# Two-item gelu, third-level sums, early output products for the last tokens, and a re-tuned planner, in an attention kernel with an MLP beside it

## Chip, cores, metric

One core of one Trainium2 chip. The metric is device time in microseconds (us) of one execution. A kernel before and a kernel after are compared on the same chip, in alternation. The profiled span is 1.7 to 2.2 us shorter than the time measured for the same execution. Engines are called PE (matmul), PEld (its weight loads), ACT (ScalarE), DVE (VectorE), POOL (GpSimd) and SP (SyncE, which issues the transfers).

## The reference

```python
# x: (1, 2048, 1024) bf16, 32 heads of 32; w1: (1024, 3584), w2: (3584, 1024)
def reference(A_x, A_wqkv, A_wo, B_x, B_w1, B_b1, B_w2, B_b2):
    xn = _layernorm(A_x)
    s = attention(xn, A_wqkv) @ A_wo                 # softmax(q k / sqrt(32)) v, all 2048 x 2048 pairs
    y = _layernorm(xn)
    h = jax.nn.gelu(y @ B_w1 + B_b1, approximate=True)
    g = jax.nn.silu(h @ B_w2 + B_b2)
    return A_x + s * g
```

## The kernel before

The attention is cut into 512 units: 8 head groups of 4 heads, 8 query blocks of 256 tokens, 8 pairs of key blocks. A unit is 8 score matmuls on PE, two exps of 128x1024 on ACT, then products with V and with a block of ones (the row sums) on PE. DVE first adds the P tiles (the results of the exps) pairwise, so that fewer products with ones are needed. The MLP and the projections fill PE's time between scores, in chunks of one or a few matmuls. An instruction that takes a finished result out of PSUM is called an evacuation; the prologue is the normalisation of x and the first projections. A Python planner, which runs when the program is built, simulates the engines with a few constants and fixes the instruction order of each engine. On the chip every engine then takes its instructions in that order.

```python
# planner: how long a transfer takes (in ns), and what issuing one costs SP
state["bw"] = max(state["bw"], t) + o.nbytes / 210.0
o.fin = state["bw"] + 1900.0
...
def dma(sem, fn, nbytes, R, W, prio=3, extra=()):
    return add("SP", fn, 70, 0, R, W, prio, sem=sem, nbytes=nbytes, extra=extra)
...
# one w1 item: 16 matmuls in chunks of two, then gelu over its 512 columns
for k in range(8):
    ...
    chunk(it, fn, 2 * Q256, [("w1", gi), ("yT", k % 4)])
dve(... xb_t[i3] = bank + b1T ...)                      # out of PSUM
dve(... sq = xb * xb ...); dve(... ut = (sq + 1/GA) * xb ...)
act(lambda e: e.activation(ut_t[i3][:], ut_t[i3][:], ACT.Tanh, scale=GC * GA), c_act(512), ...)
dve(... hT = (ut + 1) * xb ...)
...
# row sums: two levels of adds for each pair of units; either is dropped if it would be late
pa = dve(... PA[u], PA[u+1] = P[:, :, 0] + P[:, :, 1] ...)   # 2048 columns
pb = dve(... PA[u] = PA[u] + PA[u+1] ...)                    # 1024 columns
...
# output of 128 tokens x 512 columns: eight products, one evacuation, one add, one store.
# For the last 256 tokens the eighth (head group 7) is kept apart and may start first in its bank.
for hc in range(HG):
    chunk(itb if hc == 7 else it, fn, Q512, ...)
```

The softmax here doesn't subtract the row's maximum and nothing guards it: scores larger than these inputs give would overflow.

## Time and profile before

| | kernel before |
|---|---|
| time, median of 3 runs | 1062.07 us (1061.9 to 1062.5) |
| span of the profiled execution | 1060.2 us |
| end of the last exp | 1046.1 us |
| tail: last exp to last PE / PE to the end | 10.7 + 3.4 us |
| full 512-wide matmuls after the last product with V, in PE's order | 43 |

The busy shares, the chain and the stretches are shown in the prediction. Two more views: first the waits of PE, with the columns total us, times, longest us (the nine that follow these are of 0.5 to 2.2 us each, for results of DVE, POOL and ACT).

```profile
PE ps L1058 <- ACT P L1067: 8.0, 18, 1.2
PE ps L668 <- issue: 3.5, 22, 0.2
```

Then the transfers of w1, by count, size and median us from issue to landing. The planner took 524288 / 210 + 1900 = 4397 ns for one with no other ahead of it, which is the measured median as the view rounds it.

```profile
w1r<-in_B_w_dram SPq DMA_DIRECT2D x112, 512.0 KB, 4.4
```

One measure is used throughout. ACT starts its next instruction 904 ns after an exp (a copy, at 920, is counted alike), 520 after a tanh of 512 columns, 946 after one of 1024; what a start comes later than that is its lateness. From 62 us on I call a start *long late* if it is over 0.18 us late, and *brief* is the sum of all the rest. Before, long late starts make 0.2 us and brief ones 10.6; up to 62 us ACT loses 17.9 (*opening*).

### The profile page before, as it was taken

Reading aid. Unit: us, or ns where it says so; the run is one execution under the profiler, and the core shown is the slowest. Engines: PE = TensorE matmul, PEld = TensorE weight load, DVE = VectorE, ACT = ScalarE, POOL = GpSimd, SP = SyncE. Lnnn points to the kernel's source line nnn. Section 1 sums busy time; section 2 is a strip of 40 time slices with the busy share of each in tenths; the row PEclk is TensorE's granted clock in tenths of the full one; section 3 lists DMA queues with packets and bytes.
Section 4 is the critical chain, followed back from the end, with each engine's and each line's share of the span. In section 5 each row is a group of like instructions: output and inputs, shape, how many; then the busy total and the mean of one; then the engine's idle time right before and its main releaser. Section 6 shows DMA issues by size and latency. Waiting matters only on the chain.

```text
span 1060.2 us, 32647 instructions
## 1 busy us (share of the span) xinstructions
PE 1026.5 (97%) x14502; PEld 643.7 (61%) x14562; DVE 946.9 (89%) x1585; ACT 1028.9 (97%) x1186; POOL 31.2 (3%) x42
## 2 busy tenths in 40 slices
PE   7999999999999999999999999999999999999998
PEld 5756466556665566566665566466665666665443
DVE  8479898999999998899989998999999998978996
ACT  4999999999999999999999999999999999999994
POOL 5500000000000000000000000000000000000000
PEclk9999999999999999999999999999999999999999
DMA  9335166522674466423763476224765776662442
GB/s 268 111 96 158 42 179 190 144 76 71 186 207 126 113 193 196 113 57 112 206 192 105 122 199 195 74 76 121 212 180 151 221 217 190 179 197 70 134 140 87
DMA packets 285798, 156.52 MB, mean 148 GB/s; under 512 B 23642, under 2 KB 276570, under 8 KB 285658
## 3 DMA queue, kind: packets, MB, share of 16 engines
q1 hardware_dynamic: 285658, 154.44, 51.0%
q8 instruction: 114, 1.87, 0.8%
q14 instruction: 26, 0.21, 0.1%
HBM read 142.35 MB, written 12.06 MB: 146 GB/s over the span
## 4 chain that ended last, share of the span: by engine, by line
ACT 93%; PE 4%; DVE 2%; DMA 1%; issue 0%; SPq 0%; POOL 0%; POOLq 0%
ACT P L1067 86%; ACT ut L939 5%; PE ps L668 3%; ACT gw L971 2%; DVE stats L823 1%; DMA hT<-in_A_x_dram 1%; PE ps L663 1%; ACT big L814 0%; PE ps L1058 0%; PE ps L803 0%; DVE yT L911 0%; POOL gw L847 0%; DVE V L740 0%; DVE mv L825 0%; SPq L693 0%
## 5 line engine op out<-in xcount | busy, mean ns | idle before, releaser
L1067 ACT ACTIVATE P<-ps 128x1024 bf16<-128x1024 f32 x1024 | 986.8, 1243 | 5.3 <-PE ps L1058 5.3
L1087 DVE TENSOR_TENSOR PA<-P 128x2048 bf16<-128x2048 bf16 x243 | 294.7, 1215 | 25.4 <-ACT P L1067 24.1
L668 PE MATMUL ps<-yT,w1r 128*128 128x256 bf16 x1792 | 234.9, 275 | 2.3 <-DVE xb L931 1.1
L668 PE MATMUL ps<-w2r,hT 128*128 128x256 bf16 x1792 | 226.9, 273 | 0.3 <-DVE nv L1121 0.2
L668 PEld LDWEIGHTS ps<-yT,w1r 128*128 128x128 bf16 x1792 | 162.1, 98 | 60.5 <-issue 28.6
L668 PEld LDWEIGHTS ps<-w2r,hT 128*128 128x128 bf16 x1792 | 162.2, 98 | 51.0 <-issue 30.5
L1091 DVE TENSOR_TENSOR PA<-PA 128x1024 bf16<-128x1024 bf16 x219 | 147.7, 684 | 1.4
L663 PE MATMUL ps<-P,V 128*32 128x256 bf16 x4096 | 142.8, 274 | 0.6 <-DVE xb L931 0.4
L668 PE MATMUL ps<-big,qk 128*128 128x512 bf16 (+2 forms) x522 | 120.9, 357 | 5.7 <-issue 2.1
L668 PE MATMUL ps<-qk,big 128*128 128x256 bf16 (+1 forms) x723 | 121.2, 305 | 2.5 <-issue 1.3
L663 PEld LDWEIGHTS ps<-P,V 128*32 128x32 bf16 x4096 | 97.7, 96 | 33.1 <-issue 19.6
L1058 PE MATMUL ps<-QKT 32*128 32x256 bf16 x2048 | 101.7, 273 | 7.4 <-ACT P L1067 5.9
L1058 PE MATMUL ps<-qk 32*128 32x256 bf16 x2048 | 101.9, 273 | 6.2 <-ACT P L1067 2.1
L939 ACT ACTIVATE ut<-ut 128x512 f32<-128x512 f32 x112 | 94.5, 855 | 0.0
L668 PEld LDWEIGHTS ps<-qk,big 128*128 128x128 bf16 x736 | 65.3, 98 | 41.5 <-issue 13.3
L931 DVE TENSOR_TENSOR xb<-ps,b1T 128x512 bf16<-128x512 f32 x112 | 76.6, 684 | 13.9 <-PE ps L668 12.6
L941 DVE SCALAR_TENSOR_TENSOR hT<-ut,xb 128x512 bf16<-128x512 f32 x112 | 76.4, 684 | 5.9 <-ACT ut L939 5.2
L668 PEld LDWEIGHTS ps<-big,qk 128*128 128x128 bf16 x568 | 47.7, 98 | 52.4 <-issue 15.6
L1058 PEld LDWEIGHTS ps<-QKT 32*128 32x128 bf16 x2048 | 30.3, 92 | 76.6 <-ACT P L1067 75.9
L937 DVE SCALAR_TENSOR_TENSOR ut<-sq,xb 128x512 f32<-128x512 bf16 x112 | 76.1, 682 | 0.3
L1058 PEld LDWEIGHTS ps<-qk 32*128 32x128 bf16 x2048 | 30.4, 92 | 71.6 <-ACT P L1067 67.4
L663 PE MATMUL ps<-PA,ones 128*32 128x256 bf16 x1068 | 56.0, 274 | 0.3 <-DVE PA L1091 0.3
(75 smaller groups left out, 532.2 us busy)
## 6 DMA issues: line engine op xcount, KB each, us to landing
w1r<-in_B_w_dram SPq DMA_DIRECT2D x112, 512.0 KB, 4.4
w2r<-in_B_w_dram SPq DMA_DIRECT2D x128, 448.0 KB, 4.4
qk<-in_A_wqkv_dram SPq DMA_DIRECT2D x16, 256.0 KB, 3.2
g_scratch<-gw SPq DMA_DIRECT2D x32, 128.0 KB, 3.0
o_scratch<-ot SPq DMA_DIRECT2D x56, 64.0 KB, 2.8
big<-o_scratch SPq DMA_DIRECT2D x28, 128.0 KB, 3.5
hT<-in_A_x_dram SPq DMA_DIRECT2D x10, 256.0 KB, 5.5
qk<-in_A_wqkv_dram SPq DMA_DIRECT2D x4, 512.0 KB, 4.4
```

Source lines behind the costliest of these rows:

```text
L663: ins = e.matmul(dst(j), lhsT=lhsT(j), rhs=rhs(j), start=start, stop=stop, tile_position=(0, 32 * j), skip_group_check=True)
L668: return e.matmul(dst, lhsT=lhsT, rhs=rhs, start=start, stop=stop, skip_group_check=True)
L823: dve(lambda e, t=t, c=c: e.bn_stats(stats[:, t, c, :], xst[t][:, c * 512:(c + 1) * 512]), 600, [XS(t)], [("st", t, c)], 1)
L931: dve(lambda e: e.tensor_tensor(xb_t[i3][:].rearrange("p (k t) -> p k t", k=2), bank(it.bank).rearrange("p (k t) -> p k t", k=2), b1T[:, 2 ...
L937: dve(lambda e: e.scalar_tensor_tensor(ut_t[i3][:], sq_t[p % 2][:], 1.0 / GA, xb_t[i3][:], op0=ALU.add, op1=ALU.mult), c_f32(512), [("sq", ...
L939: act(lambda e: e.activation(ut_t[i3][:], ut_t[i3][:], ACT.Tanh, scale=GC * GA), c_act(512), [("ut", i3)], [("ut", i3)], 1)
L941: dve(lambda e: e.scalar_tensor_tensor(hT[:, hs].rearrange("p k t -> p (k t)"), ut_t[i3][:], 1.0, xb_t[i3][:], op0=ALU.add, op1=ALU.mult), ...
L971: act(lambda e: e.activation(zh_t[zi], z_t[zi], ACT.Tanh, scale=0.5), c_act(512), [("z", zi)], [("zh", zi)], 1)
L1058: ins = e.matmul(bank(b0[j], kk * 256, (kk + 1) * 256), lhsT=QKT[sl][32 * j:32 * j + 32, 1, kb * 128:(kb + 1) * 128], rhs=QKT[sl][32 * j:3 ...
L1067: x = act(lambda e, h=h: e.activation(P[pi][:, 2 * h:2 * h + 2].rearrange("p j k q -> p (j k q)"), ps[:, pr[h] * 1024:(pr[h] + 1) * 1024], ...
L1087: pa = dve(lambda e: e.tensor_tensor(PA_all[:, a0:a0 + 2].rearrange("p u j q -> p (u j) q"), P_all[:, p0:p0 + 2, :, 0, :].rearrange("p u j ...
L1091: pb = dve(lambda e: e.tensor_tensor(PA[a0][:], PA[a0][:], PA[a1][:], op=ALU.add), c_b16(1024), [("PA", a1)], [("PA", a0)], PBPRIO)
```

## The change

Four things at once:
- **Gelu over two w1 items**: the squares, the cubic step and the tanh work on 1024 columns instead of twice 512; the gate (silu) likewise. ACT saves fixed costs.
- **A third level of sums**: four units share one product with ones where DVE is in time.
- **The last 256 tokens**: their products of head groups 0 to 6 are made earlier and kept in f32; only the eighth product stands at the end.
- **The planner**: new constants for transfers and latencies, chunks of one matmul, three x tiles ahead of the first weights, other patience and reserve values, and a rule ("suspension") by which one item of the prologue may go ahead of an opened one.

```diff
-GRACE2 = 600     -HARD = 45    -EARLY = 6    -RESERVE = 300    -GLAST = 11    -NOPA = 24
+GRACE2 = 1200    +HARD = 40    +EARLY = 3    +RESERVE = 800    +GLAST = 13    +NOPA = 0
+FINE = 1   +XF = 3   +ADJ = 300   +PART = 5   ...
-                state["bw"] = max(state["bw"], t) + o.nbytes / 210.0
+                state["bw"] = max(state["bw"], t) + o.nbytes / 280.0
...
-            return add("SP", fn, 70, 0, R, W, prio, ...)
+            return add("SP", fn, 430, 0, R, W, prio, ...)
...
-            for k in range(8):
-                f2, dcs = k // 4, (2 * (k % 4), 2 * (k % 4) + 1)
+            for k in range(16 // FINE):
+                f2, dcs = k // (8 // FINE), [FINE * (k % (8 // FINE)) + i for i in range(FINE)]
...
-            act(lambda e: e.activation(ut_t[i3][:], ut_t[i3][:], ACT.Tanh, scale=GC * GA), c_act(512),
+            if p % 2 == 0:
+                return it
...
+            act(lambda e: e.activation(ut_t[i2][:], ut_t[i2][:], ACT.Tanh, scale=GC * GA), c_acts(1024),
...
+            add8 = dve(lambda e: e.tensor_tensor(PA[a0], PA[a0], PA[a2], op=ALU.add), c_b16(1024),
+                       [("PA", a2)], [("PA", a0)], PCPRIO)
...
+                if qb == PART:
+                    for t2 in range(2):
+                        wo_load(NQB - 1, t2)
+                        for nh in range(2):
+                            wo_item(NQB - 1, t2, nh, 0, 7)     # products of head groups 0 to 6, kept in f32
```

(Constants set side by side and cuts marked with "...".)

## The prediction

> **What bounds the kernel now.** I read the busy shares first, then the chain that ended last, then ACT's starts, then the two ends of the run.
>
> ```profile
> PE 1026.5 (97%) x14502; PEld 643.7 (61%) x14562; DVE 946.9 (89%) x1585; ACT 1028.9 (97%) x1186; POOL 31.2 (3%) x42
> ...
> ACT 93%; PE 4%; DVE 2%; DMA 1%; issue 0%; SPq 0%; POOL 0%; POOLq 0%
> ```
>
> PE and ACT tie at 97%, so busy time does not decide between them. The chain does: 93% of the span is ACT, mostly the 1024 exps. The stretches say when:
>
> ```profile
> core 0: us, PE busy (x) PEld busy (x) DVE busy (x) ACT busy (x) POOL busy (x), PEclk, DMA share, GB/s
> 12.70:62.00 49.30, 44.82 (x584) 32.64 (x585) 32.35 (x83) 41.83 (x45) 26.49 (x32) 0.97 0.48 138
> ...
> 250.00:500.00 250.00, 246.56 (x3554) 159.26 (x3559) 230.95 (x381) 250.00 (x291) 0.00 (x0) 1.00 0.50 140
> ...
> 1046.00:1060.30 14.30, 10.66 (x80) 5.00 (x79) 7.49 (x15) 0.08 (x1) 2.31 (x2) 1.00 0.21 74
> ```
>
> In the middle ACT has no idle time at all (250.00 of 250). It loses time only before 62 us, and after 1046 us it has nothing left to do. So three things set the time: how early ACT becomes dense, how much ACT work there is, and the tail after the last exp.
>
> What one ACT instruction costs is the distance between starts, not its recorded length, because neighbours overlap:
>
> ```profile
> 400.48 0.87 ACT L939 ACTIVATE ut<-ut 128x512 f32<-128x512 f32 x1
> 401.01 4.01 ACT L1067 ACTIVATE P<-ps 128x1024 bf16<-128x1024 f32 x4
> 404.62 0.91 ACT L939 ACTIVATE ut<-ut 128x512 f32<-128x512 f32 x1
> 405.14 6.80 ACT L1067 ACTIVATE P<-ps 128x1024 bf16<-128x1024 f32 x7
> ```
>
> The 512-wide tanh is recorded with 0.87 us but holds ACT for 401.01 - 400.48 = 0.53; over all such pairs in the trace the median is 520 ns for the gelu tanh and for the gate's alike. Four exps fill 404.62 - 401.01 = 3.61, or 0.90 each (median 904 ns).
>
> I also took the excess of every exp start over 904 ns. From 62.5 us on, the first exps of a pair are late 131 times for 8.2 us in all, and each late one starts about 50 ns after the last matmul of its scores: ACT waits there for PE, too briefly to show as idle. The PE work just ahead of those scores is half the time (4.1 of 8.2 us) an MLP chunk of two 256-wide matmuls.
>
> **What the Trainium skill says.** "ScalarE: Activation LUTs", section "What ACT_TABLE_LOAD costs", gives 186 ns + 0.833 ns per column for an ACTIVATE with immediate scale and bias, with neighbours overlapping by about 93 ns. That leaves 93 + 0.833 x 512 = 520 ns per 512-wide tanh: the trace agrees to the nanosecond. For the exp from PSUM it would give 946 and the trace has 904, so I use the trace there. "VectorE: DVE Perf Modes", section "Side-by-side: where the cycles go for N=2048 bf16", puts a two-times-mode bf16 operation of 2048 columns at about 1224 ns; the trace has 1215 for the sums of that size, and 684 for 1024 columns. The fixed part of one DVE instruction is therefore worth saving, but only if DVE matters. "TensorE: Matmul & The Clock Gate", section "Back-to-back issue gap", has N/2.4 + 2.5 for warm isolated matmuls, 216 ns at N=512; in the tail the trace has 215 or 216 between every two of them (the same section's 131 ns for streams is not what this trace shows).
>
> **The change, part by part.** Counts are from the order in which the two built programs stand.
>
> ACT: 112 gelu tanhs of 512 become 56 of 1024, 32 gate tanhs become 16. The columns stay; 72 fixed parts of 93 ns go: 72 x (2 x 520 - 946) = 72 x 94 ns = 6.8 us. The 946 is an estimate from the skill's formula, which held at 512. ACT is the bound where this happens, so nearly all of it should come off the end: **-6.8 us**.
>
> DVE:
>
> ```profile
> L1087 DVE TENSOR_TENSOR PA<-P 128x2048 bf16<-128x2048 bf16 x243 | 294.7, 1215 | 25.4 <-ACT P L1067 24.1
> L1091 DVE TENSOR_TENSOR PA<-PA 128x1024 bf16<-128x1024 bf16 x219 | 147.7, 684 | 1.4
> L663 PE MATMUL ps<-PA,ones 128*32 128x256 bf16 x1068 | 56.0, 274 | 0.3 <-DVE PA L1091 0.3
> L663 PE MATMUL ps<-P,ones 128*32 128x256 bf16 x208 | 7.1, 273 | 0.0
> ```
>
> First-level sums go 243 to 251, second-level 219 to 202, and 57 third-level sums are new. In distances between starts (1135 ns for 2048 columns, 602 for 1024 bf16 or 512 at the single rate, 335 for 512 bf16): +8 x 1.135 - 17 x 0.602 + 57 x 0.602 = +33.2 us. The two-item gelu gives back 56 x (2 x 0.335 - 0.602) = 3.8 for the squares, 56 x (2 x 0.602 - 1.135) = 3.9 for the cubic step, and 16 x 0.07 = 1.1 for the gate; the last gelu step stays split. DVE thus gains about 24 us of work, from 89% to some 92% busy by the page's measure. It is beside ACT, so I count **0**, but it takes slack away.
>
> PE: matmuls against ones fall from 1276 to 1052, that is 224/4 = 56 groups of four at about 0.11 us (the tail has 28 of them in some 0.8 us): 6 us less. PE is not the bound, so **0** directly. Chunks of the MLP and of V become one 256-wide matmul (0.11 us) instead of two: a score matmul can be late by one such matmul less. If that and the corrected model of latencies halve the 4.1 us behind MLP chunks and take a little of the rest: **-2.5 us**, the softest term.
>
> Start: POOL normalises without a pause from 13 to 38 us in the kernel before, and the order of those instructions is the same after, so the end of the prologue does not move. What moves is how ACT fills it. Before, 10 exps stand ahead of its last copy out of PSUM, after it 12: one pair, 1.8 us, done in time that was idle. Before, one pair also waits 1.1 us at 61 us because 12 MLP matmuls stand ahead of its scores; that should be gone, but the new order can have such a place elsewhere. **-2.5 us**.
>
> Tail:
>
> ```profile
> 1046.34 1.10 PE ps L663 x36
> 1047.43 0.16 issue
> 1047.59 9.24 PE ps L668 x42
> 1056.83 0.03 issue
> 1056.86 0.70 DVE w1r L1221
> 1057.56 0.02 issue
> 1057.58 0.43 DVE w1r L1228
> ```
>
> Making the last tokens' seven products early sounds like taking 28 matmuls out of this stretch. The order says otherwise: after the last product with V there stand 43 full matmuls before and 45 after. The early products went in front, and the products of the 256 tokens ahead of them slid behind in their place. So PE needs 2 x 0.216 = 0.43 us more, and 20 fewer matmuls with V or ones (36 to 16) save about 0.6. But the end behaves worse. The last five matmuls now finish five different output tiles within 0.86 us. DVE takes five evacuations at 0.60 from 0.82 before the last matmul's end, then one bf16 add at 0.34 and two f32 adds, the last of 0.68: -0.82 + 5 x 0.60 + 0.34 + 0.60 + 0.68 = 3.8 us after the last matmul, where before it is 58.01 - 56.82 = 1.2. The store after it takes the same 2.2 us. Together 0.4 - 0.6 + 2.6: **+2.5 us** (rounded).
>
> Sum: -6.8 - 2.5 - 2.5 + 2.5 = -9.3 us on a span of 1060.2, or 1050.9; the measured time lies 1.9 above the span (1062.07 against 1060.2), so 1052.8, which I round to 1052.5.
>
> **Rivals.** (1) DVE or the deeper chain of sums becomes a wait. A third-level sum is ready only after three dependent DVE instructions, and PE takes its order as it stands: if a sum is late, PE stops with score matmuls behind it and ACT starves. For it: DVE at 92%, and PE already waits some 3 to 4 us in total for second-level sums. Against it: the program drops 70 of 127 possible third-level sums, as it does where they would be late, and the products they feed come after most of a later exp group. This would cost 5 to 10 us: 1057 to 1062. (2) PE takes over, so that a shorter ACT stream does nothing. For it: 97% busy. Against it: PE busy is lengths that overlap, and weight loads ahead of scores wait for exps 490 times (143 us in total), so PE has room. If it were so, only the 6 us of ones would count: about 1056. (3) Finer chunks remove all late scores and the prologue closes: another -5 and -3, about 1044. (4) The tail really shortens by the 28 matmuls, 6 us: it would need the other products done before the last exp; the order speaks against it. About 1046.
>
> **Range and chances.** ACT's terms are firm, the other three are each good to 2 or 3 us, and rivals 1 and 3 pull in opposite directions: 1045 to 1059.5. Faster by over 2% means under 1040.8. The ACT floor is 1024 x 0.904 + 72 x 0.946 + 16 copies at about 0.9 = 1008, plus 8.2 before the first copy, some 8 of gaps and a tail of 14: 1038 at best, so hardly. Slower by over 2% would take a large new wait.
>
> **What would show it.** Right: 56 and 16 tanhs with 946 ns to the next start; ACT without idle time between about 50 and 1037 us; DVE near 970 us busy; last exp near 1035 to 1038; a tail of 16 to 17 us with five evacuations in a row. Wrong: a merged tanh that holds ACT for 1040 ns; exps late by more than 8 us in all; PE waiting for third-level sums just ahead of scores; a tail under 13 us.

## The result, and the profile after

The kernel after takes 1066.96 us (median of 4 runs, 1065.52 to 1067.59), the kernel before 1062.28 (4 runs, 1061.9 to 1063.47). Ratios here are the mean time of one kernel's runs over that of the other's of the same rounds, so not quite the ratio of the medians that are quoted: 1.004, with a 95% interval of 1.0023 to 1.0058. By the 2% rule that is the same; but the change was predicted to save 9.6 us (1062.07 - 1052.5) and costs about 4. The result lies outside the predicted range.

The page of the kernel after, busy shares and the chain that ended last:

```profile
PE 1024.6 (96%) x14338; PEld 637.8 (60%) x14338; DVE 977.4 (92%) x1513; ACT 1024.3 (96%) x1114; POOL 34.0 (3%) x42
...
ACT 46%; PE 45%; DVE 4%; DMA 3%; POOL 1%; issue 0%; DVEq 0%; POOLq 0%
```

The chain was 93% ACT; now 45% of it runs over PE, and 3% over transfers. The stretches (length, then busy us of PE, PEld, DVE, ACT, POOL, then PE clock, DMA share, GB/s):

```profile
250.00:500.00 250.00, 245.92 (x3527) 156.77 (x3525) 228.26 (x341) 248.37 (x272) 0.00 (x0) 1.00 0.50 141
...
750.00:967.00 217.00, 211.90 (x3062) 140.70 (x3050) 198.49 (x295) 215.23 (x236) 0.00 (x0) 1.00 0.65 188
```

ACT had no idle time in these stretches before (250.00 and 217.00 busy). Now it stands idle 1.6 and 1.8 us, and 2.8 from 62 to 250 us. PE's waits say for what:

```profile
PE ps L1116 <- ACT P L1125: 11.3, 22, 2.4
PE ps L705 <- DMA w1r<-in_B_w_dram: 6.0, 6, 1.7
PE ps L705 <- DVE xb L976: 2.3, 5, 0.8
```

The middle line is new: six times PE stands before the first matmul of a w1 item until its weights have landed. One of them in the timeline (start, length, engine, line; in brackets the idle time before it and what ended it):

```profile
908.13 1.36 PE L705 MATMUL ps<-yT,w1r 128*128 128x256 bf16 x11 [1.68 <-DMA w1r<-in_B_w_dram]
...
909.42 0.40 PE L1116 MATMUL ps<-qk 32*128 32x256 bf16 x8
...
909.87 1.02 ACT L1125 ACTIVATE P<-ps 128x1024 bf16<-128x1024 f32 x1 [1.47 <-PE ps L1116]
```

PE waits 1.68 us, works off the 11 matmuls that stand before the next scores in its order, and ACT, which needs those scores, is idle 1.47 us. It is not the only one: after five of the six waits (5.4 us) a long late start follows within 2 us, and these five make 6.1 of the 9.8 us of long late starts in this execution. The transfers themselves have not slowed, since the median is 4.5 us against 4.4. What has changed is what the planner believes: 524288 / 280 + 1900 = 3772 ns. When a weight is needed as soon as it lands, it now places PE's first matmul 0.63 us before the median landing. Taken from the traces, the time from landing to first matmul of the 112 items was 17.4 us in the median before, and once as short as 0.14 us, which is what it is when PE stands waiting; after, the median is 11.5, and ten items are at 0.14.

The merged tanh, and the second-level and new third-level sums (busy us, mean ns):

```profile
L1151 DVE TENSOR_TENSOR PA<-PA 128x1024 bf16<-128x1024 bf16 x202 | 137.9, 689 | 1.7
...
L991 ACT ACTIVATE ut<-ut 128x1024 f32<-128x1024 f32 x56 | 67.6, 1212 | 0.0
...
L1154 DVE TENSOR_TENSOR PA<-PA 128x1024 bf16<-128x1024 bf16 x57 | 39.3, 689 | 1.3
```

By distance between starts a merged tanh holds ACT for 947 ns, so the predicted 946 holds. The end of the chain (start, us, what):

```profile
1048.33 8.97 PE ps L705 x41
...
1057.32 0.69 DVE V L1266
1058.02 2.39 DVE w1r L1266 x4
1060.41 0.84 DVE V L1269
1061.25 0.60 DVEq L1356
1061.85 0.60 DVE w1r L1271
```

Five evacuations in a row, then the adds, as predicted. The last matmul ends at 1058.15 us (a group of five that starts at 1056.91 and takes 1.24), the last DVE instruction at 1061.85 + 0.60 = 1062.45: 4.3 us, not 3.8. The tail comes to 17.3 us against 14.1. The timeline of the same place shows why the one bf16 add is long:

```profile
1058.69 2.27 POOL L1271 TENSOR_TENSOR w1r<-w1r,hT 128x512 bf16<-128x512 bf16 x2 [1013.92 <-DVE w1r L1266]
...
1060.32 0.93 DVE L1269 TENSOR_TENSOR V<-V 128x512 bf16<-128x512 bf16 x1
```

It takes 0.93 us, where the same instruction took 0.42 at 1056.32 us, alone. It ends 0.29 us after POOL's two adds do (1058.69 + 2.27 = 1060.96). The Trainium skill has such a case in "SBUF — State Buffer", section "Who interferes with whom": a DVE instruction with two SBUF inputs contends with a GpSimd instruction that reads SBUF. The trace agrees, with 0.5 us; the evacuations, which have one input in PSUM, ran on beside POOL at 0.60 us each. How long one engine holds the other up is not shown here, since spans on POOL are rough.

### The profile page after: what moved, and what is told of

It reads as the page before. It is cut to its first block, busy times and chain, and to the rows that moved or that the text cites. A ratio compares the mean times of both kernels' runs of the same rounds, so it can differ in the third digit from the quotient of the medians. Undisturbed runs are those within 1.5% of the kernel's fastest.

```text
span 1064.9 us, 32134 instructions
## 1 busy us (share of the span) xinstructions
PE 1024.6 (96%) x14338; PEld 637.8 (60%) x14338; DVE 977.4 (92%) x1513; ACT 1024.3 (96%) x1114; POOL 34.0 (3%) x42
## 4 chain that ended last, share of the span: by engine, by line
ACT 46%; PE 45%; DVE 4%; DMA 3%; POOL 1%; issue 0%; DVEq 0%; POOLq 0%
ACT P L1125 43%; PE ps L705 30%; PE ps L1116 8%; PE ps L700 7%; DMA w1r<-in_B_w_dram 3%; ACT ut L991 3%; DVE ut L860 1%; DVE PA L1146 0%; ACT gw L1027 0%; POOL gw L889 0%; POOL lnp L903 0%; DMA hT<-in_A_x_dram 0%; DVE xb L976 0%; DVE V L777 0%; DVE PA L1151 0%
## 5 line engine op out<-in xcount | busy, mean ns | idle before, releaser
L1125 ACT ACTIVATE P<-ps 128x1024 bf16<-128x1024 f32 x1024 | 960.9, 1198 | 10.8 <-PE ps L1116 10.5
L1146 DVE TENSOR_TENSOR PA<-P 128x2048 bf16<-128x2048 bf16 x251 | 303.9, 1212 | 17.1 <-ACT P L1125 15.9
L705 PE MATMUL ps<-yT,w1r 128*128 128x256 bf16 x1792 | 232.4, 273 | 8.7 <-DMA w1r<-in_B_w_dram 6.0
L700 PE MATMUL ps<-P,V 128*32 128x256 bf16 x4096 | 146.0, 275 | 0.9 <-DVE V L777 0.5
L1151 DVE TENSOR_TENSOR PA<-PA 128x1024 bf16<-128x1024 bf16 x202 | 137.9, 689 | 1.7
L705 PE MATMUL ps<-big,qk 128*128 128x512 bf16 (+2 forms) x568 | 131.2, 361 | 2.6 <-DVE V L777 0.8
L705 PE MATMUL ps<-qk,big 128*128 128x256 bf16 (+1 forms) x736 | 124.9, 306 | 0.2
L989 DVE SCALAR_TENSOR_TENSOR ut<-hT,xb 128x1024 f32<-128x1024 bf16 x56 | 68.2, 1220 | 0.1
L991 ACT ACTIVATE ut<-ut 128x1024 f32<-128x1024 f32 x56 | 67.6, 1212 | 0.0
L1200 DVE STREAM_TRANSPOSE nt<-ps 128x256 f32<-128x256 f32 x64 | 28.7, 448 | 28.2 <-PE ps L700 27.9
```

What stands on the lines that cost most here:

```text
L700: ins = e.matmul(dst(j), lhsT=lhsT(j), rhs=rhs(j), start=start, stop=stop, tile_position=(0, 32 * j), skip_group_check=True)
L705: return e.matmul(dst, lhsT=lhsT, rhs=rhs, start=start, stop=stop, skip_group_check=True)
L989: dve(lambda e, r=r: e.scalar_tensor_tensor(ut_t[i2][:, r], h[:, r], 1.0 / GA, xb[:, r], op0=ALU.add, op1=ALU.mult), c_f32(r.stop - r.star ...
L991: act(lambda e: e.activation(ut_t[i2][:], ut_t[i2][:], ACT.Tanh, scale=GC * GA), c_acts(1024), [("ut", i2, 0), ("ut", i2, 1)], [("ut", i2, ...
L1125: x = act(lambda e, h=h: e.activation(P[pi][:, 2 * h:2 * h + 2].rearrange("p j k q -> p (j k q)"), ps[:, pr[h] * 1024:(pr[h] + 1) * 1024], ...
L1146: add2.append(dve(lambda e, p0=p0, a0=a0: e.tensor_tensor(PA_all[:, a0:a0 + 2].rearrange("p u j q -> p (u j) q"), P_all[:, p0:p0 + 2, :, 0 ...
```

## The experiments

All sixteen runs were correct. Every call ran on one chip beside the kernel before (median 1060.84, 1060.79, 1060.72 and 1061.53 us, 7 to 9 runs each). The columns: span; end of the last exp; tail as PE + rest; lateness in the opening; long late starts from 62 to 110 us and after 110; PE's waits for w1; full matmuls after the last product with V; ratio to the kernel before with its interval. "-" is none in the list of waits.

| | span | last exp | tail | opening | long late, to 110 / after | w1 waits | left | ratio |
|---|---|---|---|---|---|---|---|---|
| before | 1060.2 | 1046.1 | 10.7+3.4 | 17.9 | 0.0 / 0.2 | - | 43 | 1 |
| after | 1064.9 | 1047.6 | 10.5+6.8 | 17.4 | 2.5 / 7.3 | 6.0 | 45 | 1.0040 [1.0023, 1.0058] |
| e1 | 1061.6 | 1044.3 | 10.5+6.8 | 20.5 | 1.0 / 1.6 | - | 45 | 1.0027 [1.0012, 1.0042] |
| e2 | 1065.2 | 1047.9 | 10.5+6.8 | 17.7 | 2.3 / 6.9 | 3.6 | 45 | 1.0049 [1.0034, 1.0064] |
| e3 | 1072.4 | 1053.4 | 12.2+6.8 | 16.6 | 1.4 / 10.4 | 4.0 | 52 | 1.0121 [1.0104, 1.0139] |
| e4 | 1067.6 | 1043.8 | 17.0+6.8 | 16.3 | 3.3 / 3.1 | 1.7 | 75 | 1.0092 [1.0077, 1.0108] |
| e5 | 1058.5 | 1041.2 | 10.5+6.8 | 17.5 | 1.1 / 2.0 | 0.6 | 45 | 1.0012 [0.9995, 1.0029] |
| e6 | 1063.5 | 1048.1 | 10.5+5.0 | 18.1 | 2.5 / 6.8 | 5.1 | 45 | 1.0043 [1.0028, 1.0058] |
| e7 | 1062.0 | 1046.7 | 11.4+3.8 | 17.4 | 2.0 / 6.3 | 4.4 | 48 | 1.0043 [1.0026, 1.0061] |
| e8 | 1058.3 | 1043.1 | 11.4+3.9 | 17.4 | 2.9 / 1.9 | 1.0 | 48 | 0.9994 [0.9979, 1.0009] |
| e9 | 1066.9 | 1043.9 | 19.1+3.9 | 19.0 | 1.6 / 1.6 | - | 85 | 1.0068 [1.0053, 1.0083] |
| e10 | 1067.8 | 1046.8 | 17.6+3.4 | 18.2 | 0.3 / 1.0 | 1.8 | 75 | 1.0080 [1.0065, 1.0095] |
| e11 | 1063.2 | 1042.6 | 17.2+3.4 | 17.7 | 2.1 / 1.0 | - | 73 | 1.0019 [1.0002, 1.0036] |
| e12 | 1063.3 | 1045.2 | 11.4+6.8 | 16.8 | 1.9 / 5.1 | 2.4 | 48 | 1.0061 [1.0040, 1.0081] |
| e13 | 1063.0 | 1045.8 | 10.5+6.8 | 17.3 | 2.8 / 5.0 | 2.1 | 45 | 1.0038 [1.0024, 1.0052] |
| e14 | 1059.1 | 1043.7 | 10.5+4.9 | 16.6 | 3.7 / 2.9 | 0.6 | 45 | 1.0003 [0.9991, 1.0016] |
| e15 | 1056.6 | 1042.4 | 10.3+3.9 | 16.7 | 1.0 / 2.8 | - | 43 | 0.9970 [0.9957, 0.9982] |
| e16 | 1057.5 | 1043.4 | 10.3+3.9 | 18.5 | 1.1 / 2.1 | - | 43 | 0.9969 [0.9956, 0.9981] |

The theory: PE waits for w1 because the planner was told a faster transfer rate. The rivals, tested beside it: the start with three x tiles, the merged tanh itself, the third-level sums, the end.

### e1: the old rate in the changed kernel

```diff
-                state["bw"] = max(state["bw"], t) + o.nbytes / 280.0
+                state["bw"] = max(state["bw"], t) + o.nbytes / 210.0
```

> Only the transfer rate that the planner assumes goes back from 280 to 210 bytes per ns, so that it counts 4.4 us and not 3.8 for the landing of a 512 KB piece of the first MLP weight (the trace has 4.4 to 4.5). Theory (the plan now asks for those weights too early): PE's waits for that weight fall from 6.0 us in six places to under 1.5, the exp starts that are late by over 0.5 us after 62 us (8 of them, 9 us together) mostly go, and the time falls by 4 to 8 us, to 1059 to 1063. Rival (third-level sums or finer chunks hold PE): no change, 1065 to 1068. The tail after the last exp stays at 16 to 18 us under both.

1063.76 us, ratio 1.0027. The waits for w1 are gone, and long late starts fall from 9.8 to 2.6 us. The time gained only 0.13%, not the 4 to 8 us expected, in part because the opening became 3.1 us worse (20.5 against 17.4): with 210 the planner thinks the first transfers slower than they are and orders the prologue badly. PE then waits there for POOL's normalised tokens 4.8 us instead of 1.6:

```profile
PE ps L840 <- POOL gw L889: 4.8, 2, 2.9
```

So in the changed kernel one constant does two jobs: 280 fits the opening, when transfers run back to back (267 GB/s in the first of the 40 slices of its page), and 210 the middle. In the kernel before, the opening hardly depends on it (17.9 with 210, 18.2 with 280 in e10).

### e2: two x tiles ahead of the first weights

```diff
-XF = 3
+XF = 2
```

> Only the order of the first loads goes back: two tiles of x ahead of the first weights, not three. Theory (the third tile gives DVE two more statistics ahead of the first tile's normalisation): the first copy out of PSUM starts near 8.2 us instead of 9.1 and the first exp near 12.7 instead of 13.8; the time falls by about 1 us if nothing else in the plan moves, and by less or more where it does. Rival (start is set by the weights or POOL): first exp unchanged. The waits for the first MLP weight stay (5 to 8 us), so 1064 to 1068.

1066.16 us, ratio 1.0049. The first exp moves from 13.77 to 12.15 us, and the same 31 exps have begun by 62 us. The start is no cause, and what is won at the first exp does not reach the end. (Part of the 1.6 us is chance: in e13, the unedited program, the first exp starts at 12.93.)

### e3: the gelu tanh as two of 512 again

```diff
-            act(lambda e: e.activation(ut_t[i2][:], ut_t[i2][:], ACT.Tanh, ...), c_acts(1024), ...
+            for j, r in enumerate(parts):
+                act(lambda e, r=r: e.activation(ut_t[i2][:, r], ut_t[i2][:, r], ACT.Tanh, ...), c_acts(512), ...
```

> Only the gelu tanh is cut back into two of 512 columns (56 of 1024 become 112 of 512); the gate's stays merged. Theory (ACT is still what most of the time hangs on, and the merge did save 93 ns a piece): ACT gets 56 x 93 = 5.2 us more work and the time rises by 4 to 6 us, to about 1072. Rival (PE sets the time now, as ACT carries only 46% of the chain): the time stays within 1.5 us of 1067.

1074.25 us, ratio 1.0121, or 8.6 us more than the change as it is (0.0081 x 1062), where 4 to 6 were expected. The two profiled executions differ by 7.5 us. The saving of the merged tanh is real: 56 x 93 ns = 5.2 us are the fixed parts; the tail is 1.7 longer (seven more matmuls, 52 against 45), long late starts are 2.0 more (11.8 in all against 9.8), and opening and brief lateness are 0.8 and 0.7 less.

### e4: no third-level sums

```diff
+            if u >= NOPA:
+                plan.skip.append(add8)
+                oc.occ += Q256
```

> Only the third-level sums are left out: PE multiplies two second-level sums with the ones instead (57 DVE additions less, 228 more matmuls against ones, some 6 us of PE). Rival 1 of the prediction (the deeper chain of sums and a busier DVE hold PE and with it ACT): DVE falls to about 940 us busy and the time falls by 3 us or more. Theory (they are harmless and also worth nothing, as neither DVE nor PE's products sets the time): within 2 us of 1067.

1070.1 us, ratio 1.0092, 5.5 us more than with them. DVE has less work (943.9 us busy against 977.4), and still it is slower. The last exp ends earlier, at 1043.8, but 75 full matmuls are left for the tail instead of 45. The chain of this kernel:

```profile
1044.47 15.44 PE ps L705 x71
```

So the third level, which I had counted as zero, is worth some 5 us in this plan. The 228 products with ones that it saves are 57 groups of four at 0.11 us, or 6 us of PE, and the 30 full matmuls that are left in its place are 6.5 us.

### e5: 280 up to 40 us, 210 from there

```diff
-                state["bw"] = max(state["bw"], t) + o.nbytes / 280.0
+                state["bw"] = max(state["bw"], t) + o.nbytes / (280.0 if t < 40000.0 else 210.0)
```

> The planner assumes 280 bytes per ns for transfers issued in its first 40 us and 210 after that. Theory (280 fits the opening, where only loads run, and 210 fits the middle; with 210 throughout, the opening was ordered worse by 3 us while the waits for weights went): the opening is as in the changed kernel (some 31 exps begun by 62 us), PE waits under 1.5 us for the first MLP weight, exps late by over 0.18 us add up to under 4 us after 62 us instead of 10, last exp near 1041, tail still 17: span 1057 to 1060, which is 4 to 8 us less than the changed kernel and about equal to the kernel before. Rival (the gain of the lower rate was chance of another order): late exps stay near 10 us.

1061.83 us, ratio 1.0012: 3.0 us (0.28%) better than after, less than the 4 to 8 expected, and no longer told from the kernel before. One wait for w1 is left, of 0.6 us. PE's two longest are

```profile
PE ps L1116 <- ACT P L1125: 11.5, 27, 1.1
PE ps L705 <- issue: 3.2, 20, 0.2
```

and the opening stays at 17.5. The two jobs of the constant are thus taken apart.

### e6 and e7: the end

e6 puts the four one-product items of the last tokens ahead of the last two items of the tokens before, so that evacuations overlap with matmuls:

```diff
+                        if lastq:
+                            q = plan.queues["wo"]
+                            q.insert(len(q) - 3, q.pop())
```

> The changed kernel with its four one-matmul products of the last tokens placed two items earlier in the queue, ahead of the last two products of the tokens before, nothing else. Theory (the tail is long because five evacuations and three additions stand in a row on DVE after the last matmul): PE ends as before, 10.5 us after the last exp, but the rest of the tail falls from 6.8 to 4 to 5 us, the time by 2 to 3 us. Rival (the tail is set by the stores): it stays at 6.5 to 7 us after PE's end. Last exp unchanged at about 1047.6.

e7 takes the early products out, so that the last tokens have eight products in one item like all others:

```diff
...
-                        wo_item(qb, t2, nh, 7 if lastq else 0, 8)
+                        wo_item(qb, t2, nh, 0, 8)
...
-                if qb == PART:
+                if False:
```

> The changed kernel without the early products: the last 256 tokens get their eight products in one piece, and nothing is kept in f32 (the four stores at the end are two of double size). Theory (the early products only change places with others; PE has about the same work left after the last exp): 48 full matmuls after the last exp instead of 45, so PE ends 11 us after it instead of 10.5, and the rest falls from 6.8 to about 3.5 us: tail 14 to 15 us instead of 17.3, time lower by 2 to 3 us. If the early products do what they were made for, the tail grows instead, by up to 28 matmuls or 6 us, to over 20 us.

1065.55 and 1065.21 us, both 1.0043. In the profiled executions the tail falls by 1.8 and 2.1 us; the measured times, where 2 to 3 us less were expected, do not show it, and with intervals of 1.6 to 1.9 us to each side they could hardly. A use of the early products is not shown either: without them 48 full matmuls are left instead of 45, three at 0.22 us, and the end after the last matmul is 3.0 us shorter.

### e8: two rates, and no early products

(The edits of e5 and e7.)

> Both edits together: two transfer rates and no early products. If both theories hold they add, as one acts before the last exp and one after it: last exp near 1041, tail 14 to 15, span near 1055.5, that is 5 us (0.5%) under the kernel before and 9 to 10 under the changed one. If the shorter ACT stream only leaves PE more work for the end, the tail stays at 17 or more and the span at 1058 or more.

1060.39 us, ratio 0.9994. Against e7, which differs only in the rate, that is 4.8 us by the medians. It misses what was expected (last exp near 1041, span near 1055.5) by some 2 us before the last exp: long late starts still make 4.8 us there.

### e9: the changed work under the old planner

```diff
-GRACE2 = 1200; HARD = 40; EARLY = 3; RESERVE = 800; GLAST = 13; PJC = 16; PJD = 10; FINE = 1; XF = 3; ADJ = 300
+GRACE2 = 600; HARD = 45; EARLY = 6; RESERVE = 300; GLAST = 11; PJC = 12; PJD = 7; FINE = 2; XF = 2; ADJ = 0
-  ... 280.0 / 52.5 / 430 / TL + 30 / 262144 * 3 // 2, suspension, early products
+  ... 210.0 / 49 / 70 / TL / 262144, no suspension, no early products
```

(The second pair of lines is in shorthand.)

> The changed kernel's work (two-item gelu and gate, third-level sums) with the planner's constants of the kernel before (rate 210, issue 70 ns, old latencies, pairs of matmuls as chunks, two tiles of x first) and no early products. By its order 85 full matmuls stand after the last product with V, against 43 before and 45 in the changed kernel. Theory (PE shares the bound: what ACT saves comes back as PE work left for the end, unless the plan places it better): few waits for weights (under 2 us), last exp at 1038 to 1040, but a tail near 85 x 0.216 + 4 = 22 to 23 us, span 1060 to 1063. Rival (ACT alone is the bound): span near 1053.

1068.29 us, ratio 1.0068: slower than the whole change, but for another reason. There is no wait for w1, and the last exp ends at 1043.9, but 85 matmuls are left. (The tail was expected so; the last exp came some 4 us later than expected, with the opening 1.1 and long late starts 3.0 us worse than before.) The old constants, which suit the old work, are no fallback for the new: the plan must be tuned for the work it orders.

### e10: the new rate alone, in the kernel before

```diff
-                state["bw"] = max(state["bw"], t) + o.nbytes / 210.0
+                state["bw"] = max(state["bw"], t) + o.nbytes / 280.0
```

> The kernel before with only the planner's transfer rate raised from 210 to 280. Theory (too high a rate makes PE meet the first MLP weights before they land): waits for that weight of 3 us or more (0 before), exps late by over 0.18 us summing to 4 us or more after 62 us (0.2 before), last exp 2 us or more later in respect of its work; 75 full matmuls instead of 43 stand after the last product with V, which is a tail of some 20 to 21 us: time above 1064. Rival (the rate is harmless by itself): late exps stay under 1 us.

1069.56 us, ratio 1.008. The rate alone costs 8.5 us (0.8%), but not in the way my theory had it. There are waits for w1,

```profile
PE ps L668 <- DMA w1r<-in_B_w_dram: 1.8, 2, 1.0
```

but only two of them, and long late starts come to 1.3 us (before: 0.2). The harm is in the tail, with 75 full matmuls left instead of 43:

```profile
1048.29 10.74 PE ps L668 x49
1059.03 0.05 issue
1059.08 5.36 PE ps L668 x24
```

A wrong constant does not only make waits where it is wrong; it deals PE's work out differently over the whole run. Which of the two it does depends on the rest of the plan.

### e11: the two-item gelu and gate alone, in the kernel before

The diff is the gelu and gate part of the change with its buffers, and nothing of the planner but a constant for the tanh of 1024:

```diff
-            act(lambda e: e.activation(ut_t[i3][:], ut_t[i3][:], ACT.Tanh, ...), c_act(512), ...
+            act(lambda e: e.activation(ut_t[i2][:], ut_t[i2][:], ACT.Tanh, ...), c_acts(1024), ...
```

> The kernel before with the two-item gelu and gate alone, all else and the planner's constants as before. ACT has 72 x 93 ns = 6.7 us less. If ACT is the bound (the prediction's first term): time down by 5 to 7 us, to about 1055. If PE shares it: last exp earlier by 5 to 7 us, near 1040, but 73 full matmuls instead of 43 after the last product with V, so a tail of 20 to 21 us instead of 14.1: time within 2 us of the kernel before.

1063.49 us, ratio 1.0019: 72 fixed parts of ACT, 6.7 us, are saved, and the time is no better. Two things ate it. ACT got 3.1 us of long late starts (before: 0.2), so the last exp ends 3.5 us earlier and not 6.7. And the tail is 6.5 us longer, because 73 full matmuls are left. (Some 2 us of this are PE's own: the planner drops 17 second-level sums more, and so has 68 products with ones more.) The chain:

```profile
1042.82 1.10 PE ps L666 x36
1043.92 0.16 issue
1044.08 10.74 PE ps L671 x49
1054.82 0.05 issue
1054.87 4.92 PE ps L671 x22
```

PE ends at 1059.8, later than before (1056.8), with ACT done earlier: PE's work bounds the end as well as ACT's.

### e12: chunks of two matmuls in the changed kernel

```diff
-FINE = 1
+FINE = 2
```

> The changed kernel with chunks of two 256-wide matmuls, as before, instead of one. The prediction gave 2.5 us to the finer chunks through exps that wait briefly (under 0.18 us each) for their scores; the changed kernel has 9.7 us of such waits and the kernel before 10.6. Theory (finer chunks are worth at most 1 us there): these brief waits add up to 10 to 11.5 us. If they were worth what was predicted: 12 us or more. The time stays within 2 us of the changed kernel, with its waits for weights.

1067.05 us, ratio 1.0061; its interval overlaps that of the kernel after. Brief lateness is 10.6 us here and 9.7 with the fine chunks: in brief lateness they are worth 0.9 us, not 2.5.

### e13 and e14: the change again, and with both mends

e13 is the kernel after without an edit, for its spread; e14 has the edits of e5 and e6.

> The changed kernel, unedited, as the yardstick for the next three on one chip. As before: ratio to the kernel before 1.003 to 1.005, waits for the first MLP weight of 4 to 7 us, tail 17.3 us.

> Two transfer rates (280 to 40 us, 210 after) and the one-matmul products two items earlier. Theory: the edits add, as one acts before the last exp (3 to 6 us) and one after it (1.8 us): last exp 1041 to 1043, tail 15.5, time 5 to 7 us under the changed kernel, 0.998 to 1.000 of the kernel before. Rival (the profiles that showed it were lucky executions): under 3 us.

1065.1 us, ratio 1.0038, and 1061.13, ratio 1.0003: the mends bring 3.7 us (0.35%) on one chip, less than expected. e13 also shows how far one execution is from another: with the same program its waits for w1 are 2.1 us in three places, against 6.0 in six, and its long late starts after 110 us 5.0, against 7.3.

### e15 and e16: plans tuned for this work

Both have two rates (280, then 205) and no early products; the other constants were picked from many builds by the planner's own computed end.

```diff
# e15
+GRACE2 = 1600; HARD = 48; RESERVE = 300; GLAST = 11; AGE_A = 1500; AGE_D = 1800; PJB = 14; PJC = 12; PJD = 12
# e16
+EARLY = 2; RESERVE = 500; GRACE3 = 1500; ADJ = 450; PJB = 14; AGE_A = 700
```

> Two rates (280 to 40 us, 205 after), no early products, and other planner constants, picked because the planner then ends earliest. 43 full matmuls stand after the last product with V, as many as in the kernel before. If the ACT saving is kept out of the tail, the last exp is at 1040 to 1042 and the tail 14 to 14.5: time 4 to 6 us under the kernel before (ratio 0.994 to 0.997). If new waits take it: ratio 0.998 or more.

> As the tuned kernel a, with another set of constants (also 43 matmuls left). The same is expected: ratio 0.994 to 0.997 if it holds generally and not for one lucky order, with last exp at 1040 to 1042 and a tail of 14 to 14.5 us.

1058.28 and 1057.28 us, ratios 0.9970 and 0.9969, at the weak end of what was expected. Both are faster than the kernel before by 0.3% and faster than the kernel after by some 7 to 8 us. The end of e16's chain:

```profile
1044.30 9.40 PE ps L705 x43
1053.70 0.02 issue
1053.73 0.70 DVE w1r L1266
```

ACT is done at 1043.4, and 43 matmuls are left: both engines end earlier together (PE by 3.1 us, at 1053.7 against 1056.8). What is not shown is that the 0.3% belongs to the new work: no run gave the kernel before constants from such a search.

## Why the prediction was wrong

The account of the last exp in the kernel after closes: 1046.1 - 6.7 (tanh) - 0.5 (opening) - 0.9 (brief) + 9.6 (long late) = 1047.6, as measured. The tail adds 3.2. Against the predicted -9.3 the span moved +4.7; the 14.0 between them are:

| term | predicted | measured | miss |
|---|---|---|---|
| ACT's fixed parts | -6.8 | -6.7 | 0.1 |
| late scores behind chunks | -2.5 | -0.9 | 1.6 |
| start | -2.5 | -0.5 | 2.0 |
| tail | +2.5 | +3.2 | 0.7 |
| long late starts (no such term) | 0 | +9.6 | 9.6 |

**The step that failed.** It is "ACT is the bound where this happens, so nearly all of it should come off the end", with its sign in the profile, "ACT without idle time between about 50 and 1037 us". The 6.8 was right. But that ACT is dense was a property of the old order, not of the engine, and I carried it over to an order that the diff itself had planned with other constants. In that order ACT stood waiting for PE: +9.6 us of long late starts from 62 us on, where the prediction had none. The diff shows the rate going from 210 to 280, the page showed 4.4 us for a w1 piece, and dividing one by the other would have shown that the old number fits and the new one does not. No rival was a wait for a transfer.

**How much of the 9.6 is the rate.** After 110 us, five executions planned with 280 (after, e2, e6, e7, e13) have 7.3, 6.9, 6.8, 6.3 and 5.0 us of long late starts, mean 6.5; four with 210 there (e1, e5, e8, e14) have 1.6, 2.0, 1.9 and 2.9, mean 2.1. That makes 4.4 us. (The runs left out of these means, with other edits, are e3, e4 and e12 with 280, at 10.4, 3.1 and 5.1, and e9, e15 and e16 with 205 or 210, at 1.6, 2.8 and 2.1: the two groups still do not overlap, but e4 comes near.) The measured times agree: the pairs that differ in the rate alone gain 3.0 us (after to e5), 5.2 (e7 to e8), 4.2 (e6 to e14, each by its ratio), and e1 1.4 in spite of an opening worse by 3.1. So the rate is shown for some 4 us, and with it the sign of the result: with it mended the change is level with the kernel before.

**What stays open of it.** Long late starts from 62 to 110 us are 1.0 to 3.7 us in all sixteen traces with the two-item gelu, and 0.0 and 0.3 in the two without it (before, e10). e11, which adds the two-item gelu and gate alone, has 2.1. So they come with it in these runs, though in the kernel after 1.1 of its 2.5 us follow a wait for w1 (at 91.75 us). In the trace of e11 PE stands there before an evacuation that DVE does late, behind gelu steps that wait for their tanh; no run tested that. The last 2 us after 110, scattered, are not settled. So of the 14.0 us of the miss, some 4 are shown by an edit to come from the rate, some 5 of the long late starts stay open, and the rest are sizes read from the traces.

**ACT and PE bound together.** My second rival, PE as the bound, I weighed at "about 1056" and set aside since PE's weight loads wait 143 us for exps. It was nearer than my own sum. e11 makes ACT's work shorter and not PE's: nothing is gained. e4 keeps the shorter ACT and takes the third level away: 5.5 us are lost, and in the profiled executions the last exp is even 3.9 us earlier and the tail 6.5 longer. e3 keeps the third level and lengthens the tanhs: 8.6 us are lost. Of the runs made, only those with both and a plan that fits (e15, e16) end earlier, by 0.3%; e11's work under a plan tuned for it was not run. In counting the tanh in full and the products with ones as 0, I treated the end as a single engine's.

**The softer terms.** Fine chunks were worth 0.9, not 2.5 (e12): they let a score be late by one matmul less, but new orders make new late places. At the start the ones that I counted on were not won: 31 exps have begun by 62 us before and after. The tail's mechanism was right (the early products only change places with others, five evacuations stand in a row), and of the 0.7 too little 0.5 is the add beside POOL and 0.3 the last store (2.5 us after DVE's end, not 2.2).

**Right.** DVE: 977.4 us busy, "near 970" predicted; it did not become the bound, and before its products with sums PE stood idle 0.1 us in all. (The "3 to 4 us" that PE was said to wait for second-level sums before were the waits of weight loads, 3.3 us; the matmuls themselves waited 0.5.) The tail was 17.3 us, just above the "16 to 17" predicted. The time is within 2% of before, as predicted, but on the other side.

## What to carry to other kernels

When a program is ordered by a model at build time, read a change of the model's constants like a change of the program: put each next to the duration that the old profile shows, per stage, and ask what will wait if it is too fast. An engine that is dense in the old profile need not be so in a new order. And where two engines are 97% busy, count the work of both up to the end: here, shortening one alone moved work into the tail.

## What the Trainium skill lacked or had wrong

- "ScalarE: Activation LUTs", section "What ACT_TABLE_LOAD costs": 93 + 0.833 x 1024 = 946 ns between starts is right for a tanh of 1024 columns from SBUF (947 measured), as it was for 512 (520). For the exp of the same width from PSUM to bf16 it is 42 ns too much (904 measured); that section does not tell a source in PSUM from one in SBUF, though the skill does so elsewhere.
- "TensorE: Matmul & The Clock Gate", section "Back-to-back issue gap": its 131 ns for sustained products of 512 columns appears nowhere here: no two starts lie nearer than 215 ns in the traces of before, after and e4, and 41 products in the tail took 8.97 us. The section's formula for isolated ones (216 ns) is what held.
- "DMA: Bandwidth & Descriptors", section "Measured (HBM→SBUF, 128 partitions, SWDGE, issued from GpSimd)": its figures, like the page's fitted formula, are for transfers issued from GpSimd. What mattered, the time from issue to landing of a 512 KB weight piece issued from SyncE amid other transfers, it lacks: 4.4 to 4.5 us median, 5.5 to 5.6 at the 90th percentile, 9.7 to 10.4 at worst, in two traces.
